# Batch 1's first two row tiles as seven half-size products, and the weight differences for them earlier

## The chip, the core and the metric

The kernel runs on one core of one Trainium2 chip. Such a core has several engines that run their own instruction streams at the same time and meet only at semaphores: TensorE (matrix products; PE in the profile, with PEld for its weight loads), VectorE (DVE), ScalarE (ACT), GpSimd (POOL) and SyncE (SP, which here issues DMAs). Products land in PSUM, which has eight banks; all other tiles are in SBUF. The metric is the device time of one execution in microseconds (us). It was 298.46 us before the change, the median of three runs from 298.05 to 299.08.

## The reference, cut to what matters

The program is block-sparse attention followed by a mixing layer, for four batches of 768 tokens, eight heads of 64.

```python
scores = scale * np.matmul(q, k.transpose(0, 1, 3, 2))
scores = np.where(mask, scores, -1000000000.0)      # blocks: window, first, last, sampled
attn = np.exp(scores - max); attn = attn / attn.sum()
x = np.matmul(attn, v)                              # [4, 768, 512] over all heads
a1 = alpha1 * x + beta1
u = x + lam * np.einsum('ts,bsd->btd', w_tok, a1)   # tokens mixed
a2 = alpha2 * u + beta2
ch = np.maximum(a2 @ w_ch1, 0.0) @ w_ch2            # 512 -> 2048 -> 512
out = u + lam * ch
```

The change is about the last product, `relu(...) @ w_ch2`, with 2048 rows of weights and 512 columns.

## The kernel before, in words

**Units and groups.** A batch has four pairs of heads, so there are 16 pairs, numbered from 0. For each pair the scores are computed transposed (keys on the partitions) in nine *units* of 128 x 1024; a unit's scores are matrix products on TensorE (L601), an exp on ScalarE (L619), from pair 5 on a multiplication by the 0/1 mask on VectorE (L636, "mask" below), and then the products with v on TensorE (L671, "PV", 12 matmuls for one set of keys of one head). A PV accumulates in the single bank named `op`. When all of a head is there, VectorE takes the reciprocal of the sums (L688) and writes the scaled result to x (L689), which frees that bank. GpSimd, for the last head VectorE, then computes a1 (L705, L706).

**The layer's jobs.** Once a batch is ready, its layer is done in small jobs. An *f* (`job_f1`, L919) is four matmuls of 384 columns into one PSUM bank and a Relu on ScalarE (L926), which writes one of 16 rows of h for one half of the tokens; the halves are called c = 0 (token tiles 0, 1, 2) and c = 1 (tiles 3, 4, 5). A *g* (`job_f2`, L1058) is four matmuls of 512 columns, a quarter of the second product of one token tile; the fourth is followed by an addition to x on VectorE (L1067) and a store (L1071, issued by SP). A token product (`job_tok2`, L846) is followed by an addition (L858) and casts (L865) on VectorE.

**The order is written out by hand.** From pair 5 on, each string of W1, W2, W2L and W3 is one *group* of three units. Group n below is the n-th string of W1 followed by W2 and W2L, counted from 0; so groups 0 to 8 belong to pairs 5 to 7, groups 9 to 20 to pairs 8 to 11 and groups 21 to 32 to pairs 12 to 15. Each letter is one step, emitted in that order: `q` the products of the group's three units and the first exp, `x` one further exp, `k` one mask, `p` one PV, `f` and `g` one job of that kind, `T` a token product, `A` two rows of a difference of weights (`job_t`), `S` a sum or difference of rows of h (`job_s`), and others for loads and transposes. The engines execute their own instructions in the order in which these letters put them; nothing is reordered afterwards. An `f` with no job ready does nothing.

**PSUM banks.** Three banks (`mm`) serve the f, g, T, and the first unit of each group (two banks at once); two pairs of banks (`sp`) serve the other two units. A new user of a bank waits for the last reader of the user before it: for an f that is the Relu, for a score unit the exp, for a g the addition.

**Half-size products.** Batches 2 and 3 already compute part of the second product for two token tiles at once, as a quad (`job_p`, L1170): the two tiles by the two halves of the 2048 rows, against w2's four quarters, with seven products of half the columns in place of eight (the Winograd form of Strassen's method). One such product is eight matmuls of 256 columns. It needs four differences of w2's quarters, T1 to T4 (`job_t`, L1098, 16 VectorE instructions in all, in the space of q and k tiles that are no longer used), and four sums or differences of the rows of h (`job_s`, L1144: S1 and S2 write new tiles, S3 and S4 overwrite h). Each of the seven products is followed by an addition to x on VectorE (L1180). Products 1, 6 and 5 share a bank one after the other, and so do 7 and 4. The two tiles of a quad are t and t + 3.

Of the kernel before, what the change touches and what calls it, by code (L numbers as in the profile page):

```python
# [18 lines left out]
B = 4  # L19
H = 8  # L20
S = 768
# [4 lines left out]
DM = 512  # L26
P = 128
NT = S // P
# [13 lines left out]
POUR = [-19, 2, 2]  # L42
W1 = [
# [9 lines left out]
]  # L53
W2 = [
# [12 lines left out]
]  # L67
W2L = [
# [18 lines left out]
]  # L87
STR = (2, 3)
HN = NH // 2
HC = DM // 2  # L90
FS = 6
# [157 lines left out]
def kernel(  # L249
# [16 lines left out]
    nc = tc.nc  # L266
# [194 lines left out]
    def sp_tile():  # L461
        return psum.tile([P, 2, 512], FP, name="sp", tag="sp", bufs=2)
# [111 lines left out]
    x_sbs = {}  # L574
# [234 lines left out]
    did = set()  # L809
# [3 lines left out]
    hts = {}  # L813
# [301 lines left out]
    def a_of(b, t, name, r=slice(0, HN)):  # L1115
        if name in ("X1", "X2"):
            return xs[(b, t, name)][:, r]
        c, half = {"11": (0, 0), "12": (0, 1), "21": (1, 0), "22": (1, 1)}[name]
        return hts[(b, c)][:, HN * half + r.start : HN * half + r.stop, ts(t, P)]

    SOP = {
        1: ("X1", "21", "22", ALU.add),
# [5 lines left out]
    def job_s(b, t, n, r=slice(0, HN)):  # L1128
        dst, a, c, op = SOP[n]
        rows = range(r.start, r.stop)  # L1130
        for name in (a, c):
            if name[0] == "X":
                assert all(("S", b, t, int(name[1]), m) in did for m in rows)
            else:
                h, half = divmod(int(name) - 11, 10)
                assert all(("f", b, h, HN * half + m) in did for m in rows)
# [7 lines left out]
        nc.vector.tensor_tensor(  # L1144
            out=a_of(b, t, dst, r), in0=a_of(b, t, a, r), in1=a_of(b, t, c, r), op=op
        )
        did.update(("S", b, t, n, m) for m in rows)
# [8 lines left out]
        7: ("21", "T3", 3),  # L1156
    }
    banks = {}

    def mul(b, t, n, ps, start, cols=slice(0, HC)):  # L1160
        a, m, need = PROD[n]
        assert m in bq or all((m, r) in did for r in range(0, HN, 2))
        if need:
            assert all(("S", b, t, need, r) in did for r in range(HN))
        c, half = {"1": (0, 0), "X": (1, 0)}.get(a[0], (1, 0))
        if need == 0:
            h, half = divmod(int(a) - 11, 10)
            assert all(("f", b, h, HN * half + r) in did for r in range(HN))
        for r in range(HN):
            nc.tensor.matmul(  # L1170
                ps,
                a_of(b, t, a)[:, r],
                b_rows(m, r)[:, 0, cols],
                start=(start and r == 0),
                stop=(r == HN - 1),
                skip_group_check=True,
            )

    def plus(x, ps):
        nc.vector.tensor_tensor(out=x, in0=x, in1=ps, op=ALU.add)  # L1180

    def twice(ps):
        return ps.unsqueeze(1).broadcast_to([P, 2, HC])

    lo, hi = slice(0, HC), slice(HC, DM)

    def job_p(b, t, n):
        x = x_sbs[b]
        last = (b, t) == (B - 1, NT // 2 - 1)
        bk = banks.setdefault((b, t), {})  # L1190
        if n in (1, 2, 7):
            bk[n] = sp_tile()[:, 0] if n == 1 else mm_tile()[:]
        if n == 3 and not last and 2 not in bk:
            bk[2] = mm_tile()[:]
        if n == 1:
            mul(b, t, 1, bk[1][:, lo], True)
            plus(x[:, t, lo], bk[1][:, lo])
        elif n == 2:
            mul(b, t, 2, bk[2][:, lo], True)
            if last or b < B - 1:  # L1200
                plus(x[:, t, lo], bk.pop(2)[:, lo])
            if last:
                emit_store(b, t, lo)
        elif n == 6:
            mul(b, t, 6, bk[1][:, lo], False)
            plus(x[:, t + 3, lo], bk[1][:, lo])
        elif n == 7:
            mul(b, t, 7, bk[7][:, lo], True)
            plus(x[:, t + 3, hi], bk[7][:, lo])
        elif n == 5:  # L1210
            mul(b, t, 5, bk[1][:, lo], False)
            plus(x[:, t : t + 4 : 3, hi], twice(bk[1][:, lo]))
        elif n == 4:
            mul(b, t, 4, bk[7][:, lo], False)
            plus(x[:, t + 3, lo], bk[7][:, lo])
            emit_store(b, t + 3, slice(0, DM))
        elif last:
            for h in range(2):
                sl = slice(HC + h * P, HC + h * P + P)
                ps = (mm_tile(), op_tile([P, DM]))[h]  # L1220
                mul(b, t, 3, ps[:, sl], True, ts(h, P))
                plus(x[:, t, sl], ps[:, sl])
                emit_store(b, t, sl, (nc.sync, nc.scalar)[h])
        else:
            sl = hi if b < B - 1 else slice(0, DM)
            mul(b, t, 3, bk[2][:, hi], b < B - 1)
            plus(x[:, t, sl], bk[2][:, sl])
            emit_store(b, t, slice(0, DM))
        did.add((b, t, n))

    NPAIR = B * NP
# [34 lines left out]
    def start_mlp(b):  # L1266
# [16 lines left out]
        ]  # L1283
        todo["S"] += [lambda t=t, n=n, r=r: job_s(b, t, n, r) for t, n, r in S_ORDER[b]]

    REST = (6, 7, 5, 4, 3)
    P_ORDER = {
        2: [(0, g, "g") for g in range(4)]
        + [(t, 2) for t in (1, 2)]
        + [(3, g, "g") for g in range(4)]  # L1290
        + [(t, 1) for t in (1, 2)]
        + [(t, n) for t in (1, 2) for n in REST],
        3: [(t, n) for t in range(2) for n in (1, 2)]
        + [(t, n) for t in range(2) for n in REST]
        + [(2, n) for n in (1, 2) + REST],
    }
    ALL, R1, R2 = slice(0, HN), slice(0, HN // 2), slice(HN // 2, HN)
    S_ORDER = {
        2: [(t, n, ALL) for t in (1, 2) for n in (1, 2, 3, 4)],
        3: [(t, n, R1) for n in (1, 2, 3) for t in range(3)]  # L1300
        + [(t, n, r) for t in range(3) for n, r in ((1, R2), (2, R2), (3, R2), (4, ALL))],
    }

    def start_pair(i):
# [227 lines left out]
```

## Time and profile before

| What | us |
|---|---|
| median of the runs | 298.46 |
| the profiled execution, its own time | 298.76 |
| its span in the trace | 297.1 |
| TensorE busy | 289.7 (98%) |
| VectorE busy | 237.8 (80%) |
| ScalarE busy | 217.1 (73%) |
| GpSimd busy | 109.8 (37%) |

The span runs from the first to the last instruction of the trace; the profiled execution's own time is 1.66 us longer. A matmul's end is modelled in this profile and successive matmuls overlap, so TensorE's busy time says less than the distance from one start to the next. The starts of the groups of interest, by their first L601: group 1 at 63.08, group 10 at 105.14, group 15 at 134.56, group 16 at 142.44, group 17 at 148.73, group 18 at 154.89, group 19 at 159.38, group 20 at 164.88, group 21 at 170.21 and group 22 at 173.69 us. In rows of the timeline a bracket at the end gives the idle time of the engine before the instruction and what ended it.

### The profile page before, as it was taken

What the parts mean: (1) busy time and instruction counts of PE and PEld (TensorE: products, weight loads), DVE (VectorE), ACT (ScalarE), POOL (GpSimd) and SP (SyncE); (2) the same over time, 40 slices, a digit from 0 to 9 for tenths busy, and PEclk for the clock granted to TensorE, in tenths of its full rate; (3) what the DMA queues carried; (4) which work ended last, traced back from release to release, by engine and by line L of the source; (5) the groups of instructions that cost most, each with busy time, mean ns of one, the idle gap of its engine ahead of it and who ended that gap; (6) DMA issues with size and microseconds to landing.
All of it is one profiled execution on the core that took longest, in us unless ns stands there. A gap on an engine that the chain in (4) does not pass through costs nothing.

```text
span 297.1 us, 7554 instructions
## 1 busy us (share of the span) xinstructions
PE 289.7 (98%) x3082; PEld 193.5 (65%) x3101; DVE 237.8 (80%) x485; ACT 217.1 (73%) x324; POOL 109.8 (37%) x149
## 2 busy tenths in 40 slices
PE   8999999999999999999999999999999999999995
PEld 3688888665567565565576466556576679665884
DVE  4988899995678796977878777895956899799774
ACT  4999999998899963999779581999869744576000
POOL 8997978632443710355323340335320300000000
PEclk9999999999999999999999999999999999999999
DMA  6999999992392995729955767745520211400032
GB/s 182 184 199 186 192 171 187 171 123 44 95 147 55 112 203 84 118 65 119 125 96 73 124 110 146 103 92 69 70 62 17 38 38 29 141 1 3 0 141 73
DMA packets 57274, 31.09 MB, mean 105 GB/s; under 512 B 37204, under 2 KB 54016, under 8 KB 57240
## 3 DMA queue, kind: packets, MB, share of 16 engines
q0 software_dynamic: 16752, 14.22, 34.4%
q1 hardware_dynamic: 40020, 15.92, 29.3%
q8 instruction: 24, 0.39, 0.6%
q10 hardware_dynamic: 468, 0.47, 0.5%
q14 instruction: 10, 0.08, 0.1%
HBM read 29.75 MB, written 6.29 MB: 121 GB/s over the span
## 4 chain that ended last, share of the span: by engine, by line
PE 84%; DVE 6%; DMA 4%; ACT 3%; issue 1%; POOL 1%; SPq 0%; POOLq 0%
PE mm L919 18%; PE mm L1058 13%; PE sp L601 10%; PE mm L846 8%; PE op L671 7%; PE mm L1170 5%; PE sp L1170 4%; PE mm L601 3%; DVE eT L636 3%; PE mm L822 3%; PE op L648 2%; DMA vr<-in_v_dram 2%; ACT eT L619 2%; PE mm L1016 2%; PE sp L1016 2%; DMA uraw<-ubf 2%
## 5 line engine op out<-in xcount | busy, mean ns | idle before, releaser
L619 ACT ACTIVATE eT<-sp,expb 128x1024 f16<-128x1024 f32 x111 | 118.4, 1120 | 2.1 <-PE sp L601 1.4
L636 DVE TENSOR_TENSOR eT<-eT,mask 128x1024 f16<-128x1024 f16 x99 | 80.6, 843 | 13.5 <-ACT eT L619 13.3
L919 PE MATMUL mm<-uT,w1b 128*128 128x384 bf16 x416 | 76.8, 326 | 0.4 <-ACT hts L926 0.3
L705 POOL TENSOR_TENSOR a1pp<-x_sb,vbc 128x384 bf16<-128x384 f32 x25 | 28.5, 1138 | 119.0 <-DVE x_sb L689 84.7
L619 ACT ACTIVATE eT<-mm,expb 128x512 f16<-128x512 f32 x66 | 41.7, 685 | 26.5 <-PE mm L601 26.3
L926 ACT ACTIVATE hts<-mm 128x384 bf16<-128x384 f32 x104 | 49.1, 502 | 13.3 <-PE mm L919 12.4
L919 PEld LDWEIGHTS <-w1b 128*128 128x128 bf16 x416 | 38.7, 98 | 26.4 <-issue 2.9
L1058 PE MATMUL mm<-w2b,hts 128*128 128x512 bf16 x205 | 52.2, 379 | 0.9 <-issue 0.2
L671 PEld LDWEIGHTS <-eT 128*128 128x128 f16 x792 | 29.8, 98 | 8.8 <-issue 1.7
L1058 PEld LDWEIGHTS <-hts 128*128 128x128 bf16 x224 | 19.8, 98 | 22.3 <-issue 3.9
L671 PE MATMUL op<-vext,eT 128*128 128x65 f16 x792 | 32.1, 194 | 0.4 <-DVE x_sb L689 0.3
L601 PE MATMUL sp<-qTs,kTs 88*128 88x512 bf16 (+1 forms) x120 | 26.9, 325 | 1.2 <-ACT eT L619 0.7
L706 POOL TENSOR_TENSOR a1pp<-a1pp,vbc 128x384 bf16<-128x384 bf16 x25 | 26.7, 1069 | 2.0
L846 PE MATMUL mm<-a1pp,wtokT 128*128 128x256 bf16 x216 | 25.9, 273 | 0.1
L846 PEld LDWEIGHTS <-wtokT 128*128 128x128 bf16 x216 | 20.6, 98 | 5.6 <-issue 1.8
L1170 PEld LDWEIGHTS <-hts 128*128 128x128 bf16 x208 | 19.5, 98 | 3.0 <-issue 0.3
L858 DVE TENSOR_TENSOR x_sb<-x_sb,mm 128x512 f32<-128x512 f32 x18 | 12.3, 686 | 9.9 <-PE mm L846 9.8
L601 PE MATMUL sp<-qhT,khT 64*128 64x256 bf16 (+1 forms) x176 | 19.8, 322 | 0.0
L601 PEld LDWEIGHTS <-khT 64*128 64x128 bf16 x264 | 10.6, 94 | 12.7 <-issue 9.2
L648 PEld LDWEIGHTS <-eT 128*128 128x128 f16 x360 | 14.9, 97 | 3.8 <-issue 0.3
L689 DVE TENSOR_TENSOR x_sb<-op,rcp 128x384 f32<-128x384 f32 x28 | 15.6, 558 | 1.0
L1067 DVE TENSOR_TENSOR x_sb<-x_sb,mm 128x512 f32<-128x512 f32 x14 | 9.6, 686 | 8.2 <-PE mm L1058 6.7
(135 smaller groups left out, 376.9 us busy)
## 6 DMA issues: line engine op xcount, KB each, us to landing
out_dram<-x_sb SPq DMA_DIRECT2D x23, 256.0 KB
qpad<-in_q_dram POOLq DMA_DIRECT2D x15, 192.0 KB, 4.6
kr<-in_k_dram POOLq DMA_DIRECT2D x15, 192.0 KB, 5.3
vr<-in_v_dram POOLq DMA_DIRECT2D x15, 192.0 KB, 6.3
w1b<-in_moe_w_ch_dram POOLq DMA_DIRECT2D x4, 512.0 KB, 9.2
w2b<-in_moe_w_ch_dram POOLq DMA_DIRECT2D x4, 512.0 KB, 7.7
hts<-in_moe_w_tok_dram POOLq DMA_DIRECT2D x2, 576.0 KB, 8.7
x_sb<-in_k_dram ACTq DMA_DIRECT2D x2, 192.0 KB
```

What stands on the lines that cost most here:

```text
L601: nc.tensor.matmul(sp[jj][:, dst], lhsT, rhs, start=True, stop=True, skip_group_check=True,)
L619: nc.scalar.activation(dst, at, AF.Exp, bias=expb[:], scale=SCALE)
L636: nc.vector.tensor_mul(out=e, in0=e, in1=keep)
L648: nc.tensor.matmul(op[0][:, o, :], ets[u][:, jj, h * QB + n * P : h * QB + n * P + P], vexts[i % NVB][:, w, 2 * jp + jj, :], start=op[1] == 0,
L671: nc.tensor.matmul(op[0][:, o, :], ets[u][:, jj, h * QB + n * P : h * QB + n * P + P], vexts[i % NVB][:, w, 2 * jp + jj, :], start=op[1] == 0,
L705: eng.tensor_tensor(out=dst, in0=x_sbs[b][:, :, cols], in1=bc[0], op=ALU.mult)
L706: eng.tensor_tensor(out=dst, in0=dst, in1=bc[1], op=ALU.add)
L846: nc.tensor.matmul(ps[:, o], wtokT[:, os_, ts(2 * n + o, P)], a1pps[i][:, os_, :], start=(os_ == 0 and o == 0), stop=(os_ == NT - 1 and o ...
L919: nc.tensor.matmul(ps[:, 0:QC], w1b[:, dk, ts(n, P)], uTs[b][:, dk, ts(c, QC)], start=(dk == 0), stop=(dk == 3),)
L926: nc.scalar.activation(h_row(b, c, n), ps[:, 0:QC], AF.Relu)
L1058: nc.tensor.matmul(ps[:], ht[:, nk, ts(o % 3, P)], w2b[:, nk, :], start=(nk == 0), stop=(nk == NH - 1),)
L1170: nc.tensor.matmul(ps, a_of(b, t, a)[:, r], b_rows(m, r)[:, 0, cols], start=(start and r == 0), stop=(r == HN - 1), skip_group_check=True,)
```

## The change

Batch 1 joins the batches with half-size products, with one quad of its tiles 0 and 1; tiles 2 to 5 stay as they were. A quad is now named by its two tiles, so that both may lie in the half c = 0; the quads of batches 2 and 3 are the same as before under the new names, and product 1 of the new quad uses an `mm` bank where theirs uses an `sp` bank.

- Eight g of batch 1 go (groups 15, 16, 19 and 20), seven half-size products come: product 2 at the end of group 17, products 1 and 6 in group 18, products 5, 7 and 4 in group 19, product 3 in group 20. S1 is in group 15, S2 in group 16, S3 and S4 in group 18.
- The f of batch 1 come earlier: groups 15 and 16 have nine and six in place of seven and four, the last is in group 19 in place of 21, and the g of tile 2 and later are one letter later or earlier.
- The 16 letters A leave groups 14, 15 and 18 for groups 1 (three), 3 (two), 4 (three), 5 (three), 7 (one), 8 (two) and 9 (two).

```diff
 W1 = [
-    "q Y 0 f 1 k p 2 x f f f x f k k p f g",
+    "q Y 0 f 1 k A A A p 2 x f f f x f k k p f g",
...
-    "q K x g p k 0 k 1 x Q p L Y f f g 2 g k",
-    "q g g x x 0 1 f k 2 k f p k p",
-    "q 0 s 1 s k x x p T f 2 k f k p",
+    "q A A K x g p k 0 k 1 x Q p L Y f f g 2 g k",
+    "q A A A g g x x 0 1 f k 2 k f p k p",
+    "q A A A 0 s 1 s k x x p T f 2 k f k p",
...
-    "q f 0 1 x s f T 2 f L d k k x f k f p p",
-    "q 0 x p x g k k 1 d g k g 2",
+    "q f 0 1 x s f T 2 f L d k A k x f k f p p",
+    "q A A 0 x p x g k k 1 d g k g 2",
 ]
 W2 = [
-    "q 0 p p g k x L x p f k 1 K 2 k",
+    "q A A 0 p p g k x L x p f k 1 K 2 k",
...
-    "q k 0 f x f p s f f x 1 L p k 2 f f f k Y A A A A A f",
-    "q f L f 0 f k A A A A A A A A 1 f Y x f p g x f p f g k k 2",
-    "q x k x k Q 0 g 1 s f f g p 2 p f f k p",
-    "q T 0 k f 1 x k f T x f 2 p k K p",
-    "q A A A x 0 x T k 1 k f 2 k f Q f d p L",
-    "q x 0 x K k g d k s f g f 1 k p p g 2",
-    "q Y g x x k g k f 0 1 k 2 p g v g v",
+    "q k 0 f x f p s f f x 1 L p k 2 f f f k Y f",
+    "q f L f 0 f k 1 f f S Y x f p f x f p f k k 2",
+    "q x f k x f k Q 0 1 s f f p 2 p f f k S p",
+    "q T 0 k f 1 x k f T x f 2 p k K p g",
+    "q S S g x 0 x T k g 1 k f 2 k f Q d p L",
+    "q x 0 x K k g d k s g f 1 k p p g 2",
+    "q Y g x x k g k 0 1 k 2 p v g v",
 ]
 W2L = [
-    "q 0 p p g k x L x p f k 1 K 2 k",
+    "q 0 p p g k x L x p g k 1 K 2 k",
...
-STR = (2, 3)
+STR = (1, 2, 3)
...
+    LATE = [(2, (1, 4)), (2, (2, 5))] + [(3, (o, o + 3)) for o in range(3)]
...
-        if n in (1, 2, 7):
-            bk[n] = sp_tile()[:, 0] if n == 1 else mm_tile()[:]
+        if n == 1 and (b, t) in LATE:
+            bk[1] = sp_tile()[:, 0]
+        elif n in (1, 2, 7) or (n == 3 and not tail):
+            bk[n] = mm_tile()[:]
...
     P_ORDER = {
+        1: quad((0, 1), (2, 1, 6, 5, 7, 4, 3)) + direct(2, 3, 4, 5),
...
     S_ORDER = {
+        1: [((0, 1), n, ALL) for n in (1, 2, 3, 4)],
```

The letter `g` stands for the next of the batch's second-product jobs, whichever kind it is.

More of the change, by code (lines that the diff above doesn't have):

```diff
@@ L1117, in a_of, with a_ready @@
             return xs[(b, t, name)][:, r]
-        c, half = {"11": (0, 0), "12": (0, 1), "21": (1, 0), "22": (1, 1)}[name]
-        return hts[(b, c)][:, HN * half + r.start : HN * half + r.stop, ts(t, P)]
+        o, half = t[int(name[0]) - 1], int(name[1]) - 1
+        return hts[(b, o // 3)][:, HN * half + r.start : HN * half + r.stop, ts(o % 3, P)]
+    def a_ready(b, t, name, rows):
+        if name[0] == "X":
+            return all(("S", b, t, int(name[1]), m) in did for m in rows)
+        o, half = t[int(name[0]) - 1], int(name[1]) - 1
+        return all(("f", b, o // 3, HN * half + m) in did for m in rows)
     SOP = {
@@ L1130, in job_s @@
         rows = range(r.start, r.stop)
[L1131 to L1136, printed above, removed]
+        assert a_ready(b, t, a, rows) and a_ready(b, t, c, rows)
         if n == 3:
@@ L1164, in mul @@
             assert all(("S", b, t, need, r) in did for r in range(HN))
[L1165 to L1168, printed above, removed]
+        assert a_ready(b, t, a, range(HN))
         for r in range(HN):
@@ L1221, in job_p @@
                 mul(b, t, 3, ps[:, sl], True, ts(h, P))
-                plus(x[:, t, sl], ps[:, sl])
-                emit_store(b, t, sl, (nc.sync, nc.scalar)[h])
-        else:
[L1225 to L1228, printed above, removed]
+                plus(x[:, o1, sl], ps[:, sl])
+                emit_store(b, o1, sl, (nc.sync, nc.scalar)[h])
+        else:
+            assert {(b, t, m) for m in (1, 2, 5)} <= did
+            sl, ps = (slice(0, DM), bk[2]) if tail else (hi, bk[3])
+            mul(b, t, 3, ps[:, hi], not tail)
+            plus(x[:, o1, sl], ps[:, sl])
+            emit_store(b, o1, slice(0, DM))
         did.add((b, t, n))
@@ L1284, in start_mlp, with direct, quad @@
         todo["S"] += [lambda t=t, n=n, r=r: job_s(b, t, n, r) for t, n, r in S_ORDER[b]]
+    def direct(*tiles):
+        return [(o, g, "g") for o in tiles for g in range(4)]
+    def quad(t, order):
+        return [(t, n) for n in order]
     REST = (6, 7, 5, 4, 3)
     P_ORDER = {
[L1288 to L1295, printed above, removed]
+        1: quad((0, 1), (2, 1, 6, 5, 7, 4, 3)) + direct(2, 3, 4, 5),
+        2: direct(0)
+        + quad((1, 4), (2,))
+        + quad((2, 5), (2,))
+        + direct(3)
+        + quad((1, 4), (1,))
+        + quad((2, 5), (1,))
+        + quad((1, 4), REST)
+        + quad((2, 5), REST),
+        3: quad((0, 3), (1, 2))
+        + quad((1, 4), (1, 2))
+        + quad((0, 3), REST)
+        + quad((1, 4), REST)
+        + quad((2, 5), (1, 2) + REST),
     }
     ALL, R1, R2 = slice(0, HN), slice(0, HN // 2), slice(HN // 2, HN)
+    Q3 = [(0, 3), (1, 4), (2, 5)]
     S_ORDER = {
[L1299 to L1301 removed]
+        1: [((0, 1), n, ALL) for n in (1, 2, 3, 4)],
+        2: [(t, n, ALL) for t in ((1, 4), (2, 5)) for n in (1, 2, 3, 4)],
+        3: [(t, n, R1) for n in (1, 2, 3) for t in Q3]
+        + [(t, n, r) for t in Q3 for n, r in ((1, R2), (2, R2), (3, R2), (4, ALL))],
     }
```

26 lines of the change are left out of this document (13 added, 13 removed).

## The prediction

> **What bounds the kernel now.** I read the engine totals, then busy time by stretch, then the rows in order of time around the change. Group n is the n-th string of W1 followed by W2, counted from 0; f, g and PV are the jobs named in the section on the kernel. From the page's engine totals and the busy time by stretch (columns: stretch, its length, busy us of PE, PEld, DVE, ACT, POOL with instruction counts, clock, DMA share, GB/s):
>
> ```profile
> PE 289.7 (98%) x3082; PEld 193.5 (65%) x3101; DVE 237.8 (80%) x485; ACT 217.1 (73%) x324; POOL 109.8 (37%) x149
> ```
> ```profile
> 63.08:105.14 42.06, 41.85 (x441) 25.29 (x445) 31.14 (x55) 37.54 (x57) 18.24 (x20) 1.00 0.72 95
> 134.56:154.89 20.33, 20.23 (x203) 12.91 (x204) 15.45 (x33) 16.29 (x27) 7.87 (x9) 1.00 0.94 124
> ```
>
> The first stretch is groups 1 to 9, the second groups 15 to 17. TensorE has almost no idle time in either, at full clock, while VectorE and ScalarE have a fifth of the second free. The profile models where a matmul ends, so I price each kind by its pace, start to start, in the chain that ended last (start us, length us, what):
>
> ```profile
> 54.76 1.30 PE mm L919 x8
> 114.19 1.73 PE mm L1058 x8
> 251.13 0.87 PE sp L1170 x8
> ```
>
> That is 0.163 us for 384 columns, 0.216 for 512, 0.109 for 256: an f (four) is 0.65, a g (four) 0.86, a half-size product (eight) 0.87. The timeline of groups 15 and 16 shows these paces without holes:
>
> ```profile
> 135.32 3.42 PE L919 MATMUL mm<-uT,w1b 128*128 128x384 bf16 x20
> 138.58 0.53 PE L671 MATMUL op<-vext,eT 128*128 128x65 f16 x12
> 138.95 1.02 PE L1058 MATMUL mm<-w2b,hts 128*128 128x512 bf16 x3
> 141.48 1.03 PE L1058 MATMUL mm<-w2b,hts 128*128 128x512 bf16 x4
> 142.44 0.39 PE L601 MATMUL mm<-qhT,khT 64*128 64x512 bf16 x2
> 143.19 1.04 PE L1058 MATMUL mm<-w2b,hts 128*128 128x512 bf16 x4
> ```
>
> Five f take 138.58 - 135.32 = 3.26, a PV of 12 takes 0.37, the scores 0.75, and before the scores 0.09 is lost (142.44 - 141.48 - 0.87). So TensorE's order of work sets the time here: what it is spared counts, and what makes it wait counts too.
>
> **TensorE's saving.** Eight g (32 matmuls of 512) go, 6.91 us; seven products (56 of 256) come, 6.10. Saved: 0.81 us, the most that the change can give. The pace of 0.109 is of the same kind of product, one weight load for each, so the 24 more loads are in it.
>
> **The moved differences.** Sixteen L1098 instructions leave groups 14, 15 and 18. TensorE did not wait for VectorE there, so this gives nothing. In groups 1 to 9 they fill VectorE's gaps:
>
> ```profile
> 82.00 0.69 DVE L1067 TENSOR_TENSOR x_sb<-x_sb,mm 128x512 f32<-128x512 f32 x1 [2.10 <-PE mm L1058]
> 85.66 0.69 DVE L636 TENSOR_TENSOR eT<-eT,mask 128x1024 f16<-128x1024 f16 x1 [1.16 <-ACT eT L619]
> ```
> ```profile
> L1098 DVE TENSOR_TENSOR qTs<-w2b 128x512 bf16<-128x512 bf16 x4 | 1.4, 409 | 0.0
> L1144 DVE TENSOR_TENSOR xs<-hts 128x1024 bf16<-128x1024 bf16 x2 | 1.4, 682 | 0.0
> L1180 DVE TENSOR_TENSOR x_sb<-x_sb,mm 128x256 f32<-128x256 f32 x15 | 6.2, 417 | 1.4 <-PE mm L1170 1.4
> ```
>
> Three of 0.41, overlapping by 0.07, are 1.1 us: inside 2.10 (group 4) and 1.16 (group 5). In the stretch VectorE idles 42.06 - 31.14 = 10.9 us for 5.5 us of added work. I take nothing; a bound is 0.5 us, if one set of three runs late in group 5 and its delay reaches the scores of group 7, which wait for an L858.
>
> **The added VectorE work.** Four sums of 0.68 and seven additions of 0.42 (one of 512 columns, 0.69) replace two of 0.69: 4.5 us more in groups 15 to 20, partly where the differences leave. The matrix sums themselves are early enough. What is late stands in the next three parts.
>
> **First wait: groups 15 and 16.** Two g each become f, 0.43 us less for TensorE and two Relus more for ScalarE. From the timeline of ScalarE, and a hand-over where TensorE did wait:
>
> ```profile
> 138.13 0.49 ACT L926 ACTIVATE hts<-mm 128x384 bf16<-128x384 f32 x1 [0.16 <-PE mm L919]
> 138.52 1.11 ACT L619 ACTIVATE eT<-sp,expb 128x1024 f16<-128x1024 f32 x1
> 139.51 0.49 ACT L926 ACTIVATE hts<-mm 128x384 bf16<-128x384 f32 x1
> 139.88 1.13 ACT L619 ACTIVATE eT<-sp,expb 128x1024 f16<-128x1024 f32 x1
> 140.88 0.51 ACT L926 ACTIVATE hts<-mm 128x384 bf16<-128x384 f32 x1
> 142.86 1.27 ACT L619 ACTIVATE eT<-mm,expb 128x512 f16<-128x512 f32 x2 [0.69 <-PE mm L601]
> ```
> ```profile
> 127.22 0.49 ACT L926 ACTIVATE hts<-mm 128x384 bf16<-128x384 f32 x1
> 127.77 0.39 PE L601 MATMUL mm<-qhT,khT 64*128 64x256 bf16 x4
> ```
>
> An exp holds ScalarE 1.00 us, a Relu 0.37; a Relu starts 0.20 after its f's last column (137.93 to 138.13) and frees its bank 0.49 + 0.05 later. Changed group 15: scores to 135.32, nine f, two PV: TensorE is at the scores of group 16 at 141.92 + 0.09 = 142.01. Their second product needs the bank of the eighth f. ScalarE: Relu of the fifth f 138.79, exp 139.16, two Relus 140.16 and 140.53, exp 140.90, Relu of the eighth 141.90 to 142.40. TensorE waits to 142.45, 0.42 beyond the 0.03 by which that product follows. In group 16 ScalarE then does two half exps (0.57 each) from 142.64, an exp, a Relu to 145.28; the fourth f needs that bank and stands ready at 145.14: 0.19. Together 0.61. Ends: 0 (the banks come in time) and 0.9.
>
> **Second wait: scores of group 19.** The last f of group 18 now stands one PV ahead of the scores and holds a bank that they use. It is free 0.20 + 0.49 + 0.05 = 0.74 after the f; TensorE asks 0.37 + 0.09 + 0.03 after it: 0.25. Ends 0 and 0.4.
>
> **Third wait: product 4 of group 19.** It waits for the addition of product 7, which on VectorE stands behind a mask, the addition of product 5 and another mask. Rows of before, VectorE and POOL:
>
> ```profile
> 157.17 0.69 DVE L858 TENSOR_TENSOR x_sb<-x_sb,mm 128x512 f32<-128x512 f32 x1 [0.56 <-PE mm L846]
> 158.31 1.89 DVE L636 TENSOR_TENSOR eT<-eT,mask 128x1024 f16<-128x1024 f16 x3
> 160.11 0.19 DVE L688 RECIPROCAL rcp<-op 128x6 f32<-128x6 f32 x1
> 160.34 0.56 DVE L689 TENSOR_TENSOR x_sb<-op,rcp 128x384 f32<-128x384 f32 x1
> 160.97 1.00 POOL L705 TENSOR_TENSOR a1pp<-x_sb,vbc 128x384 bf16<-128x384 f32 x1 [9.22 <-DVE x_sb L689]
> 161.10 3.35 DVE L636 TENSOR_TENSOR eT<-eT,mask 128x1024 f16<-128x1024 f16 x3 [0.21 <-ACT eT L619]
> 162.05 1.25 POOL L706 TENSOR_TENSOR a1pp<-a1pp,vbc 128x384 bf16<-128x384 bf16 x1
> ```
>
> Three masks take 1.89 alone and 3.35 beside POOL's L705 and L706. In the changed order L858 to the end of L689 is 3.72 + 0.33 for the addition put among them, so L705 starts 0.20 + 4.05 + 0.07 = 4.32 after the third token product. The next mask is ready after product 6 (0.87), two f (1.30), a PV (0.37), 0.09, 0.42 to the exp (142.44 to 142.86), its halves 0.57 and 0.69, and 0.03: 4.34. A tie. If L705 starts first, the two masks take 1.49 and 0.83 instead of 0.69, each overlapping its neighbours by 0.09, and the addition of product 7 ends at 4.34 + 1.40 + 0.60 + 0.74 + 0.42 = 7.50; TensorE is there at 2.63 + 1.00 (scores with the second wait) + 0.87 + 0.87 + 0.65 + 0.74 = 6.76, and waits 0.8. If the mask starts first, it waits for nothing. I take the middle, 0.4, since the rows put the two within 0.02 of each other.
> The Trainium skill (SBUF — State Buffer, Who interferes with whom) says that a VectorE instruction with two SBUF inputs and a POOL instruction reading SBUF exclude each other, and whichever issues first holds the port for its whole length; the 3.35 against 1.89 agrees. By that rule the sum has 0 or 0.8 here, never the middle, and comes to +0.65 or +1.45.
>
> **Fourth wait: group 21.** Group 20 shrinks on TensorE, but its exps and masks stay. Before:
>
> ```profile
> 164.88 0.39 PE L601 MATMUL mm<-qhT,khT 64*128 64x256 bf16 x4
> 165.30 1.26 ACT L619 ACTIVATE eT<-mm,expb 128x512 f16<-128x512 f32 x2 [1.43 <-PE mm L601]
> 166.46 2.12 ACT L619 ACTIVATE eT<-sp,expb 128x1024 f16<-128x1024 f32 x2
> 167.31 1.99 DVE L636 TENSOR_TENSOR eT<-eT,mask 128x1024 f16<-128x1024 f16 x3
> 169.22 0.19 DVE L688 RECIPROCAL rcp<-op 128x6 f32<-128x6 f32 x1
> 169.45 0.56 DVE L689 TENSOR_TENSOR x_sb<-op,rcp 128x384 f32<-128x384 f32 x1
> 170.96 0.91 PE L671 MATMUL op<-vext,eT 128*128 128x65 f16 x24
> ```
>
> The PV of group 21 needs the single op bank, which L689 frees behind the group's last mask: 170.01 - 164.88 = 5.13 after the scores began, fixed by exps and masks. TensorE came at 6.08. Now it does scores 0.75, product 3 0.87, two g 1.73, PV 0.37, 0.09, scores 0.75 = 4.56, and waits 0.05 + 0.57 = 0.6. Ends 0.3 and 0.8.
>
> **Queues.** SP's store of tile 0 (issued in group 16 before) moves behind product 3 in group 20; a k transpose behind it goes earlier, nothing later. POOL's order is unchanged. From group 22 on all order is as before, so a shift stays to the end.
>
> **Sum.** -0.81 + 0.61 + 0.25 + 0.4 + 0.6 = +1.05 us. The profiled execution took 298.76 (span 297.1 and 1.66 around it), 0.30 above the median 298.46; on the median this is 299.5.
>
> **Rivals.**
> (1) TensorE's saving is kept whole: 298.46 - 0.81 = 297.65. For it: ScalarE has 4.0 us free in groups 15 to 17, four Relus are 1.5. Against it: the waits are of order, not of load. It decides if L689 of group 20 comes within 4.6 us of the scores and the Relu of the eighth f before the second exp; all waits together must stay under 0.81.
> (2) The mask of group 19 starts before L705: no third wait, +0.65, 299.1. The rows leave it open by 0.02. (The Trainium skill's rule above makes this a case by itself, not a shade of the forecast.)
> (3) VectorE falls behind: sums S2 or S3 meet POOL's L705 as the masks did, each 0.7 longer, before the additions that release products 1, 6 and 4: 1 us more, 300.5. Against it: L705 is due in the other part of these groups.
> (4) The early differences cost 0.5 in group 7: 300.0.
>
> **Chances.** Forecast 0.42, (1) 0.15, (2) 0.25, (3) 0.13, (4) 0.05. A change of 0.3% (0.9 us) is about what a measurement of this kernel can tell from none: below 297.56 faster, above 299.36 slower. Faster only from the low edge of (1), 0.04. Same: 0.11 of (1), 0.17 of (2), 0.15 of the forecast, 0.43. Slower 0.53. Range 298.1 to 300.4, which leaves out most of (1) and half of (3); the forecast with its own bounds is 298.9 to 300.2.
>
> **What would show it.** Right: 32 L1058 fewer, 56 half-size more at 0.109; TensorE waiting at the scores of groups 16 and 19 for Relus, at a half-size product in group 19 for an addition and at the PV of group 21 for L689; the scores of group 22 some 1 us later than 173.69 if group 15 starts as before. Wrong: no such gaps, or a start of group 15 later than 134.56.

## The result and the profile after

The changed kernel takes 300.22 us, the median of six runs from 299.94 to 300.46; beside it the kernel before took 298.66 (six runs, 298.05 to 299.08). The ratio is 1.0049 with a 95% interval of 1.0038 to 1.0061: slower by 0.5%. The prediction was 299.5 with a range from 298.1 to 300.4, on a median of 298.46. The profiled execution of the changed kernel took 300.24, with a span of 298.5.

The engine totals of the changed kernel's page, to be read against those of before (289.7, 237.8 and 217.1):

```profile
PE 291.0 (97%) x3125; PEld 196.1 (66%) x3125; DVE 242.4 (81%) x494; ACT 217.3 (73%) x324; POOL 109.8 (37%) x149
```

TensorE's share reads 97% in place of 98%, but that is rounding: 291.0 of 298.5 and 289.7 of 297.1 are both 97.5%. Its busy time rose by 1.3 us although 0.81 us of matmuls went, because this profile draws a matmul that waits as a longer one (the two L601 of group 16 take 0.83 below, those of group 21 0.39). So the totals don't show the waits. Where they are, is told by the starts of the groups, the first L601 of each, in the two profiled executions:

| Group | before, us | after, us | after minus before |
|---|---|---|---|
| 10 | 105.14 | 105.18 | +0.04 |
| 15 | 134.56 | 134.60 | +0.03 |
| 16 | 142.44 | 142.04 | -0.39 |
| 17 | 148.73 | 148.57 | -0.16 |
| 18 | 154.89 | 155.61 | +0.71 |
| 19 | 159.38 | 161.19 | +1.81 |
| 20 | 164.88 | 167.11 | +2.23 |
| 21 | 170.21 | 170.94 | +0.73 |
| 22 | 173.69 | 175.22 | +1.54 |
| 23 | 184.40 | 186.32 | +1.92 |
| 25 | 191.54 | 193.46 | +1.92 |
| 26 | 196.74 | 198.24 | +1.50 |
| 32 | 235.51 | 237.01 | +1.50 |

Up to group 15 nothing happened, from group 26 on nothing more. Between them the groups hold different work in the two kernels, so a single difference is not yet a wait. The waits are read from the changed kernel's timeline of TensorE, against the paces of the prediction (an f 0.65, a product 0.87, a PV 0.37, the scores 0.75, 0.09 ahead of a group):

```profile
142.04 0.83 PE L601 MATMUL mm<-qhT,khT 64*128 64x512 bf16 x2
142.51 0.80 PE L601 MATMUL sp<-qhT,khT 64*128 64x256 bf16 x6
143.24 2.99 PE L919 MATMUL mm<-uT,w1b 128*128 128x384 bf16 x16
146.07 0.90 PE L671 MATMUL op<-vext,eT 128*128 128x65 f16 x24
...
161.19 0.65 PE L601 MATMUL mm<-qhT,khT 64*128 64x512 bf16 x2
...
162.21 1.05 PE L1169 MATMUL mm<-qTs,xs 128*128 128x256 bf16 x8
...
164.62 0.90 PE L671 MATMUL op<-vext,eT 128*128 128x65 f16 x24
166.14 1.03 PE L1169 MATMUL mm<-kTs,hts 128*128 128x256 bf16 x8 [0.62 <-DVE x_sb L1179]
...
170.94 0.39 PE L601 MATMUL mm<-qhT,khT 64*128 64x512 bf16 x2
...
172.29 0.91 PE L671 MATMUL op<-vext,eT 128*128 128x65 f16 x24 [0.53 <-DVE x_sb L689]
...
175.22 0.39 PE L601 MATMUL mm<-qhT,khT 64*128 64x512 bf16 x2
...
176.38 1.89 PE L1058 MATMUL mm<-w2b,hts 128*128 128x512 bf16 x8 [0.34 <-ACT eT L619]
```

(A wait inside a run of equal instructions has no bracket; it shows as a distance that is too long.) The scores of group 16 take 143.24 - 142.04 = 1.20, 0.45 too long, and its four f 2.83 in place of 2.60, 0.23 too long: the first wait is 0.68. The scores of group 19 take 1.02: the second is 0.27. Product 4 starts at 166.14 where two PV from 164.62 end at 165.36: the third is 0.78. The PV of group 21 is due at 170.94 + 0.75 = 171.69 and starts at 172.29: the fourth is 0.60. And the first g of group 22 starts 1.16 after the scores in place of 0.75: a fifth wait of 0.41, for an exp, that the prediction did not have. (That exp's first half, which frees one bank, starts at 175.65; the g follows it at 176.38.) In group 25 the changed kernel gets 0.42 back (1.92 to 1.50). The four waits less the saving are 0.68 + 0.27 + 0.78 + 0.60 - 0.81 = 1.52, and group 22 starts 1.54 late; the last two nearly cancel.

The rows of VectorE and GpSimd behind the third wait, changed kernel:

```profile
162.91 1.52 DVE L636 TENSOR_TENSOR eT<-eT,mask 128x1024 f16<-128x1024 f16 x1
164.36 0.67 DVE L1179 TENSOR_TENSOR x_sb<-x_sb,mm 128x512 f32<-128x512 f32 x1
164.95 0.81 DVE L636 TENSOR_TENSOR eT<-eT,mask 128x1024 f16<-128x1024 f16 x1
165.68 0.41 DVE L1179 TENSOR_TENSOR x_sb<-x_sb,mm 128x256 f32<-128x256 f32 x1
...
162.89 1.00 POOL L705 TENSOR_TENSOR a1pp<-x_sb,vbc 128x384 bf16<-128x384 f32 x1 [11.29 <-DVE x_sb L689]
163.96 1.25 POOL L706 TENSOR_TENSOR a1pp<-a1pp,vbc 128x384 bf16<-128x384 bf16 x1
```

L705 started at 162.89 and the mask at 162.91. The mask then took 1.52, and the addition of product 7 (the last L1179) ended at 166.09, 0.05 before product 4.

### The profile page after: what moved, and what is told of

The parts are those of the page before. It is cut to its first block, busy times and chain, and to the rows that moved or that the text cites. A ratio compares the mean times of both kernels' runs of the same rounds, so it can differ in the third digit from the quotient of the medians.

```text
span 298.5 us, 7632 instructions
## 1 busy us (share of the span) xinstructions
PE 291.0 (97%) x3125; PEld 196.1 (66%) x3125; DVE 242.4 (81%) x494; ACT 217.3 (73%) x324; POOL 109.8 (37%) x149
## 4 chain that ended last, share of the span: by engine, by line
PE 85%; ACT 7%; DVE 5%; issue 1%; DMA 1%; ACTq 0%
PE mm L919 20%; PE mm L1058 13%; PE sp L601 10%; PE mm L846 8%; PE op L671 7%; PE mm L1169 6%; ACT eT L619 5%; PE sp L1169 4%; PE mm L601 3%; PE mm L822 3%; PE op L648 2%; PE mm L1016 2%; DVE eT L636 2%; PE sp L1016 2%; PE mm L648 1%; ACT hts L926 1%
## 5 line engine op out<-in xcount | busy, mean ns | idle before, releaser
L705 POOL TENSOR_TENSOR a1pp<-x_sb,vbc 128x384 bf16<-128x384 f32 x25 | 28.5, 1139 | 120.5 <-DVE x_sb L689 86.2
L1058 PE MATMUL mm<-w2b,hts 128*128 128x512 bf16 x192 | 46.7, 379 | 0.3 <-ACT eT L619 0.3
L1058 PEld LDWEIGHTS <-hts 128*128 128x128 bf16 x192 | 17.0, 98 | 18.9 <-issue 3.2
L601 PE MATMUL sp<-qTs,kTs 88*128 88x512 bf16 (+1 forms) x120 | 26.9, 325 | 1.1 <-ACT eT L619 0.7
L706 POOL TENSOR_TENSOR a1pp<-a1pp,vbc 128x384 bf16<-128x384 bf16 x25 | 26.7, 1068 | 2.0
L1169 PEld LDWEIGHTS <-hts 128*128 128x128 bf16 x248 | 23.2, 98 | 4.8 <-issue 1.8
L858 DVE TENSOR_TENSOR x_sb<-x_sb,mm 128x512 f32<-128x512 f32 x18 | 12.3, 685 | 10.6 <-PE mm L846 10.5
L601 PE MATMUL sp<-qhT,khT 64*128 64x256 bf16 (+1 forms) x176 | 20.2, 323 | 0.0
L601 PEld LDWEIGHTS <-khT 64*128 64x128 bf16 x264 | 10.9, 94 | 13.1 <-issue 9.8
L689 DVE TENSOR_TENSOR x_sb<-op,rcp 128x384 f32<-128x384 f32 x28 | 15.6, 557 | 1.0
L1179 DVE TENSOR_TENSOR x_sb<-x_sb,mm 128x256 f32<-128x256 f32 (+2 forms) x25 | 11.0, 443 | 4.0 <-PE mm L1169 3.7
```

Source lines behind the costliest of these rows:

```text
L601: nc.tensor.matmul(sp[jj][:, dst], lhsT, rhs, start=True, stop=True, skip_group_check=True,)
L705: eng.tensor_tensor(out=dst, in0=x_sbs[b][:, :, cols], in1=bc[0], op=ALU.mult)
L706: eng.tensor_tensor(out=dst, in0=dst, in1=bc[1], op=ALU.add)
L1058: nc.tensor.matmul(ps[:], ht[:, nk, ts(o % 3, P)], w2b[:, nk, :], start=(nk == 0), stop=(nk == NH - 1),)
L1169: nc.tensor.matmul(ps, a_of(b, t, a)[:, r], b_rows(m, r)[:, 0, cols], start=(start and r == 0), stop=(r == HN - 1), skip_group_check=True,)
```

## Experiments

Times are medians; beside them stands the kernel before as it ran with them.

### Only the moved differences

The kernel before with its sixteen letters A in groups 1 to 9, at the places that the change gives them:

```diff
-    "q g g x x 0 1 f k 2 k f p k p",
+    "q A A A g g x x 0 1 f k 2 k f p k p",
...
-    "q A A A x 0 x T k 1 k f 2 k f Q f d p L",
+    "q x 0 x T k 1 k f 2 k f Q f d p L",
```

> The kernel before, with only the sixteen differences of weights moved to groups 1, 3, 4, 5, 7, 8 and 9; no quad in batch 1, and the order of f and g as before. Theory (the new waits cost the time, the moved differences nothing): 298.7 us, the same as before within 0.2, and every group from 10 on starts within 0.1 us of before. Rival (the early differences delay a cast and with it the scores of group 7): 0.5 us slower, 299.2, with group 8 starting 0.5 us late.

Measured: 298.84 us beside 298.77, ratio 1.0006 (0.9998 to 1.0014). Group 0 starts 0.06 earlier than before (56.72 against 56.78), and groups 8 and 10 do too (97.78 against 97.85, 105.08 against 105.14); so does group 20 (164.81 against 164.88). So the differences cost nothing where they are now, and gave nothing where they were. Rival (4) is out.

### The changed order without the quad

The changed strings, with g in place of the seven products, the eighth g in group 20, and no sums:

```diff
-    "q S S g x 0 x T k g 1 k f 2 k f Q d p L",
+    "q g x 0 x T k g 1 k f 2 k f Q d p L",
...
-    "q Y g x x k g k 0 1 k 2 p v g v",
+    "q Y g x x k g g k 0 1 k 2 p v g v",
...
-STR = (1, 2, 3)
+STR = (2, 3)
```

> The changed kernel's order of f, g and differences in every group, but without the quad of batch 1: its seven products are g again at the same places, and the eighth g stands in group 20; the four sums and their additions are left out. Theory (the waits come from the order, except the third, which comes from the additions): the first, second and fifth wait stay, the third (0.78) goes, the added g (0.87) fills the fourth (0.58): 299.7 us, with group 20 starting 0.78 us before that of the changed kernel. Rival (the products or their sums cost more than the 0.87 each that the profile shows): groups 17 to 19 are shorter as well, and the time is 299.3 or less.

Measured: 299.61 us beside 298.50, ratio 1.0035 (1.0021 to 1.0049). Its trace runs 0.28 ahead of the changed kernel's from group 10 to group 15. Less that, group 20 starts 0.84 earlier than in the changed kernel, group 21 at the same time, and group 22 0.58 earlier: the third wait is not there, and the added g of 0.87 takes the place of the fourth. Two things follow. The order alone, without a single half-size product, costs about 1.1 us. And a product costs TensorE what a g costs: group 18 lasts 5.58 with two products (155.61 to 161.19) and 5.56 with two g (155.32 to 160.88). So the saving is the eighth g.

### The eighth Relu ahead of the exp

```diff
-    "q f L f 0 f k 1 f f S Y x f p f x f p f k k 2",
+    "q f L f 0 f k 1 f f S Y x f p f f x p f k k 2",
```

> The changed kernel with one letter moved in group 15: the eighth f stands ahead of the last exp, so that its Relu does too; TensorE's own order is the same. Theory (the first wait is one of order alone): group 16 starts 0.4 us earlier, at 142.04 still for the first product but with no gap inside its scores, the group after it 0.4 earlier, and the time is 299.8. Rival (ScalarE has nothing free across groups 15 and 16, so the exp that now comes 0.4 later makes the ninth Relu and the exps of group 16 late instead): group 17 starts within 0.15 us of where it did, and the time is 300.1 to 300.3.

Measured: 300.53 us beside 298.77, ratio 1.0056 (1.0044 to 1.0068), no better than the changed kernel's 1.0049. TensorE in group 16 of this kernel:

```profile
142.13 0.39 PE L601 MATMUL mm<-qhT,khT 64*128 64x512 bf16 x2
142.36 0.80 PE L601 MATMUL sp<-qhT,khT 64*128 64x256 bf16 x6
143.15 2.11 PE L919 MATMUL mm<-uT,w1b 128*128 128x384 bf16 x12
145.69 0.81 PE L919 MATMUL mm<-uT,w1b 128*128 128x384 bf16 x4 [0.43 <-ACT hts L926]
146.34 0.90 PE L671 MATMUL op<-vext,eT 128*128 128x65 f16 x24
```

The second product now follows the first at once. But the scores still take 1.02, and the four f take 3.19, of which 0.59 is waiting: 0.86 in all against 0.68. The rival holds: nothing was gained, and the time even lies 0.2 above its range. The likely reason is in ScalarE's timeline of the changed kernel, where no row from 139.20 to the end of the Relus at 148.14 has a bracket; ScalarE is busy 8.80 of these 8.94 us:

```profile
138.81 0.49 ACT L926 ACTIVATE hts<-mm 128x384 bf16<-128x384 f32 x1 [0.16 <-PE mm L919]
139.20 1.11 ACT L619 ACTIVATE eT<-sp,expb 128x1024 f16<-128x1024 f32 x1
...
146.17 1.97 ACT L926 ACTIVATE hts<-mm 128x384 bf16<-128x384 f32 x4
148.31 0.49 ACT L926 ACTIVATE hts<-mm 128x384 bf16<-128x384 f32 x1 [0.16 <-PE mm L919]
```

While ScalarE works without a pause, another order of its work moved the wait and did not remove it.

### Two Relus on VectorE

The Relus of the eighth f of group 15 and of the first of group 16:

```diff
+V_RELU = [(1, 1, 2), (1, 1, 4)]
...
-        nc.scalar.activation(h_row(b, c, n), ps[:, 0:QC], AF.Relu)
+        if (b, c, n) in V_RELU:
+            nc.vector.tensor_scalar_max(
+                out=h_row(b, c, n), in0=ps[:, 0:QC], scalar1=0.0
+            )
+        else:
+            nc.scalar.activation(h_row(b, c, n), ps[:, 0:QC], AF.Relu)
```

> The changed kernel with two Relus on VectorE in place of ScalarE: that of the eighth f of group 15 and that of the first f of group 16. TensorE's order is the same. Theory (the first wait is ScalarE being behind through groups 15 and 16, not the place of one Relu): the gap inside the scores of group 16 (0.42) and the 0.2 among its f go, group 17 starts 0.6 us earlier, and the time is 299.6. Rival (VectorE's masks of these groups are as late, and the two Relus push them and the scaled results behind them): group 17 gains less than 0.2, and the time is 300.1 or more.

Measured: 299.70 us beside 298.50, ratio 1.0045 (1.0029 to 1.0061), with times from 299.41 to 300.60; the profiled execution is the one of 300.60. In it the copy of v that stands ahead of the Relu on VectorE starts at 141.72, when its load has landed, against 140.38 in the changed kernel, so that the Relu starts at 142.00 and the scores wait as before. The other Relu stands behind two masks on VectorE and starts at 145.17, and the fourth f waits 0.48 for it. This one does not decide: the median points to the theory, the trace shows the rival.

### Product 2 in group 15

```diff
-    "q f L f 0 f k 1 f f S Y x f p f x f p f k k 2",
+    "q f L f 0 f k 1 f f S Y x f p f x g p f k k 2",
...
-    "q T 0 k f 1 x k f T x f 2 p k K p g",
+    "q T 0 k f 1 x k f T x f f 2 p k K p",
```

> The changed kernel with product 2, which needs no sum, in group 15 in place of the eighth f, and that f in group 17, behind the one there. ScalarE has one Relu less in groups 15 and 16, and the bank that the scores of group 16 need is freed by an addition on VectorE and not by a Relu behind an exp. Theory (the first wait, 0.61 us over both groups, is ScalarE's Relus behind its exps): the gap in the scores of group 16 goes, that among its f shrinks to 0.2 or less, so that group 18 starts 0.5 us earlier, and the time is 299.7. Rival (as with the two Relus on VectorE, the addition is itself late behind a copy that waits for a load): the gap stays, and the time is 300.1 or more.

Measured: 299.98 us beside 298.57, ratio 1.0047 (1.0032 to 1.0061). In its trace the scores of group 16 have no gap:

```profile
142.26 0.39 PE L601 MATMUL mm<-qhT,khT 64*128 64x512 bf16 x2
...
143.01 2.12 PE L919 MATMUL mm<-uT,w1b 128*128 128x384 bf16 x12
145.44 0.81 PE L919 MATMUL mm<-uT,w1b 128*128 128x384 bf16 x4 [0.30 <-ACT hts L926]
146.09 0.90 PE L671 MATMUL op<-vext,eT 128*128 128x65 f16 x24
...
142.36 0.49 ACT L926 ACTIVATE hts<-mm 128x384 bf16<-128x384 f32 x1 [0.30 <-PE mm L919]
```

The scores take 0.75, the four f 3.08, 0.48 too long. One Relu less on ScalarE has taken 0.20 off the 0.68, not the 0.5 that I expected: group 18 starts 0.19 earlier against the changed kernel, beyond a start of the trace that is 0.02 earlier. Both sides missed: the gap went, but the rest grew. The last row tells part of the reason: of the 0.37 that one Relu less frees, ScalarE spends 0.30 idle until the ninth f is done, and only from there on is it without a bracket, to the end of group 16's Relus at 148.17. The edit also has VectorE free the bank of the scores, so it does not part ScalarE's load from the choice of that bank.

### The addition ahead of the mask in group 19

```diff
-    "q x 0 x K k g d k s g f 1 k p p g 2",
+    "q x 0 x K k g d s g k f 1 k p p g 2",
```

> The changed kernel with one mask of group 19 moved behind the addition of product 7 in VectorE's order; all else is in the same order. Theory (product 4 of group 19 waits 0.78 us because that addition stands behind a mask that GpSimd's L705 and L706 lengthen): the wait before product 4 goes, group 20 starts 0.75 us earlier and the time is 299.5. Rival (VectorE is simply late there, and the mask that now comes later delays the scaled result L689 of the next group): group 20 starts 0.75 earlier, but the PV of group 21 waits that much longer, and the time stays at 300.2.

Measured: 299.77 us beside 298.77, ratio 1.0039 (1.0025 to 1.0053). Group 20 starts at 166.63, 0.52 earlier than in the changed kernel (its trace starts 0.04 later), and every later group keeps that. Timeline of TensorE, and VectorE below it:

```profile
164.68 0.90 PE L671 MATMUL op<-vext,eT 128*128 128x65 f16 x24
165.67 1.03 PE L1169 MATMUL mm<-kTs,hts 128*128 128x256 bf16 x8
...
162.97 1.52 DVE L636 TENSOR_TENSOR eT<-eT,mask 128x1024 f16<-128x1024 f16 x1
164.42 1.20 DVE L1179 TENSOR_TENSOR x_sb<-x_sb,mm 128x512 f32<-128x512 f32 x2
165.53 1.28 DVE L636 TENSOR_TENSOR eT<-eT,mask 128x1024 f16<-128x1024 f16 x2
```

Product 4 waits 0.25 where it waited 0.78. So the wait is the one named, and the rival (the next L689 late by as much) is out. A third of it stays, because the first mask, still ahead of both additions, takes 1.52; so group 20 gained 0.52 and not the 0.75 expected.

### The mask ahead of L705

```diff
-    "q S S g x 0 x T k g 1 k f 2 k f Q d p L",
-    "q x 0 x K k g d k s g f 1 k p p g 2",
+    "q S S g x 0 x T k g 1 k f 2 k Q d p L",
+    "q x 0 x K k g d k s g f f 1 k p p g 2",
```

> The changed kernel with the last f of group 18 moved to group 19, behind the one there; TensorE's work is the same. This takes away the second wait (the Relu ahead of the scores of group 19, 0.25 us), brings the scores of group 19 some 0.9 us earlier against the third token product, so that the mask is ready well before GpSimd's L705 may start, and has TensorE at product 4 as late as before. Theory of the rival with the mask first (whoever starts first decides): the mask takes 0.7 and not 1.5, the third wait goes with the second, 299.2 us. Theory that some mask of the group meets L705 or L706 whichever starts first: product 4 still waits 0.3 or more, 299.5 to 299.7. If neither wait is what I take it for, the time stays at 300.2.

Measured: 299.48 us beside 298.50, ratio 1.0034 (1.0018 to 1.0050). TensorE, VectorE and GpSimd in group 19:

```profile
160.55 0.65 PE L601 MATMUL mm<-qhT,khT 64*128 64x512 bf16 x2
...
161.57 1.05 PE L1169 MATMUL mm<-qTs,xs 128*128 128x256 bf16 x8
...
164.72 0.90 PE L671 MATMUL op<-vext,eT 128*128 128x65 f16 x24
165.45 1.04 PE L1169 MATMUL mm<-kTs,hts 128*128 128x256 bf16 x8
...
162.74 0.68 DVE L636 TENSOR_TENSOR eT<-eT,mask 128x1024 f16<-128x1024 f16 x1
163.34 0.68 DVE L1179 TENSOR_TENSOR x_sb<-x_sb,mm 128x512 f32<-128x512 f32 x1
163.94 0.90 DVE L636 TENSOR_TENSOR eT<-eT,mask 128x1024 f16<-128x1024 f16 x1
...
162.90 1.38 POOL L705 TENSOR_TENSOR a1pp<-x_sb,vbc 128x384 bf16<-128x384 f32 x1 [11.30 <-DVE x_sb L689]
```

The mask starts 0.16 before L705, takes 0.68 in place of 1.52, and it is L705 that takes 1.38 in place of 1.00. Product 4 follows the PV without a wait: the third wait is gone, and group 20 starts 0.70 earlier (at 166.42, in a trace that starts 0.01 later). The 0.08 that is missing is before the second f, which now comes 0.09 late. The second wait did not go, against what I wrote: the f that is left in group 18 still stands one PV ahead of the scores, which again take 1.02.

### A g ahead of the PV in group 21, and a g from group 22 to group 20

The first edit fills the fourth wait with a g that stood just behind it; the second brings TensorE later to that PV, and has the first g of group 22 go on in a bank that it holds:

```diff
-    "q 0 p p g k x L x p g k 1 K 2 k",
+    "q g 0 p p k x L x p g k 1 K 2 k",
```
```diff
-    "q Y g x x k g k 0 1 k 2 p v g v",
+    "q Y g x x k g g k 0 1 k 2 p v g v",
...
-    "q Q 0 g x g f v v s T T x k 1 k p p g g T g g Y d 2 k",
+    "q Q 0 g x g f v v s T T x k 1 k p p g T g g Y d 2 k",
```

> The changed kernel with one g of group 21 emitted before the first PV of that group in place of after it. Theory (TensorE waits 0.58 us there for the scaled result L689 to free the single op bank, and has a g at hand): the wait goes, group 22 starts 0.58 us earlier, and the time is 299.6 if the wait for an exp in group 22 stays as it is. Rival (group 22 is set by ScalarE and VectorE, whose exps and masks do not move): group 22 starts earlier, but its first g waits 0.4 to 0.6 us longer for the exp that frees its bank, and the time is 300.1.

> The changed kernel with one g of group 22 moved to group 20. TensorE then comes 0.87 us later to the PV of group 21, and the first g of group 22 goes on in a bank that it holds, in place of taking one that an exp of the same group must free. Theory (a fourth wait of 0.58 for L689 and a fifth of 0.38 for that exp): both go, group 23 starts 0.95 us earlier, and the time is 299.3, if the 0.42 that the changed kernel gains back in group 25 stays gained. Rival (the exp of group 22 is no wait of its own, and shows only because TensorE is early): only 0.58 goes, 299.6.

Measured, the first: 299.62 us beside 298.77, ratio 1.0027 (1.0014 to 1.0039). Group 22 starts at 174.57, 0.59 earlier than in the changed kernel beyond a start that is 0.06 earlier, and the later groups keep 0.55 of it or more. The second: 299.21 us beside 298.50, ratio 1.0025 (1.0015 to 1.0035), and group 23 starts at 185.34 where the changed kernel has 186.32, 0.98 earlier. Its TensorE in groups 21 and 22:

```profile
171.81 0.39 PE L601 MATMUL mm<-qhT,khT 64*128 64x512 bf16 x2
...
172.56 0.91 PE L671 MATMUL op<-vext,eT 128*128 128x65 f16 x24
...
175.50 0.39 PE L601 MATMUL mm<-qhT,khT 64*128 64x512 bf16 x2
...
176.25 1.90 PE L1058 MATMUL mm<-w2b,hts 128*128 128x512 bf16 x8
```

Both distances are 0.75: the fourth and the fifth wait are gone, and both theories hold to 0.03 us in the starts of the groups. The fifth wait is a wait for a bank, as the order of the letters and the exp that ends it tell. In the kernel before and in the changed one the first g of group 22 opens a tile. Before, an f closes group 21, and the new tile gets that f's bank, behind its Relu. After the change a g closes group 21 and keeps its bank until its addition; the scores of group 22 take the other two, and the new tile must have one of them back from the group's own first exp.

### All waits together

Product 2 in group 15, the f of group 18 ahead of product 6 and in group 19, and the g in group 20; in a second kernel the first Relu of group 16 also ahead of its exp, and the second f of group 19 behind a PV. Strings of groups 15 to 20 in the second kernel; group 22 as in the last diff:

```diff
-    "q f L f 0 f k 1 f f S Y x f p f x f p f k k 2",
-    "q x f k x f k Q 0 1 s f f p 2 p f f k S p",
-    "q T 0 k f 1 x k f T x f 2 p k K p g",
-    "q S S g x 0 x T k g 1 k f 2 k f Q d p L",
-    "q x 0 x K k g d k s g f 1 k p p g 2",
-    "q Y g x x k g k 0 1 k 2 p v g v",
+    "q f L f 0 f k 1 f f S Y x f p f x g p f k k 2",
+    "q f x k f x k Q 0 1 s f f p 2 p f f k S p",
+    "q T 0 k f 1 x k f T x f f 2 p k K p",
+    "q S S g x 0 x T k f g 1 k 2 k Q d p L",
+    "q x 0 x K k g d k s g f 1 k p f p g 2",
+    "q Y g x x k g g k 0 1 k 2 p v g v",
```

> The changed kernel with product 2 in group 15 as in the run beside it, the last f of group 18 in group 19 and the other one ahead of product 6, and one g of group 22 in group 20. If the five waits are independent and each goes where it was moved from (0.6 of the first, 0.27 of the second, 0.70 of the third, 0.97 of the fourth and fifth), the time is 297.7 us, 0.8 below the kernel before: the saving on TensorE is then there in full. If a wait that goes makes room for the next one behind it, 298.2 to 298.6, about the kernel before.

> The kernel of the run with all waits moved, with two letters moved: in group 16 the first f ahead of the exp that stood before it, so that its Relu comes before that exp (TensorE's order is the same), and in group 19 the second f behind one PV, so that it no longer asks for the bank of products 1, 6 and 5 before the addition of product 5 is through. Theory (that kernel still waited 0.35 for a Relu in group 16 and 0.35 for an addition in group 19, and nothing else stands behind them): both go, group 23 starts 0.7 us earlier, and the time is 297.5 us, about 1.0 below the kernel before. Rival (the exps that come 0.4 later in group 16 delay its masks and PV, and the scaled result of group 20 is next in group 21): 0.3 of it at most, 297.9.

Measured, the first: 298.14 us beside 298.57, ratio 0.9986 (0.9976 to 0.9995). The second: 297.91 beside 298.53, ratio 0.9984 (0.9975 to 0.9993). Both are a little faster than the kernel before, and both missed their expected time by 0.4, on the side of the rival. The first still waited 0.48 in group 16 and 0.36 in group 19. In the second 0.11 of the wait in group 19 is left, before product 4, but that in group 16 only went behind the PV (two PV from 145.33 end at 146.07, 0.47 before the next row):

```profile
142.72 2.77 PE L919 MATMUL mm<-uT,w1b 128*128 128x384 bf16 x16
145.33 0.90 PE L671 MATMUL op<-vext,eT 128*128 128x65 f16 x24
146.54 1.46 PE L919 MATMUL mm<-uT,w1b 128*128 128x384 bf16 x8 [0.30 <-ACT hts L926]
```

The same happened with the eighth Relu. As in the run with product 2 in group 15, ScalarE idles 0.30 until its ninth Relu, here at 142.07, and has no bracket from there to the end of group 16's Relus at 147.87.

## Why the prediction was right, and by how much it was short

The direction and the range held, at the upper edge: 300.22 is 0.02 above the forecast's own upper bound of 300.2. Step by step:

- **TensorE's saving, 0.81.** Right in size: 32 L1058 went (their weight loads fall from 224 to 192), 56 half-size matmuls came, and group 18 shows two products at the length of two g (5.58 against 5.56).
- **The moved differences, nothing.** Right, measured alone: 1.0006. Rival (4) falls with it.
- **First wait, 0.61.** It measured 0.68, at the places named. The walk found group 16 at 142.01; it started at 142.04 in a trace 0.04 later. The reason given there, the order of two Relus, was too narrow, and so was "the waits are of order, not of load": of the 13.97 us of groups 15 and 16 in the changed kernel ScalarE is busy 12.95. Three runs point to that load: another order left the wait at 0.86 in place of 0.68 or put it behind the PV, and one Relu less left 0.48. But no run removed this wait, so its cause is argued and not shown.
- **Second wait, 0.25.** It measured 0.27. It went in the two runs with all waits moved, where the f stands ahead of product 6.
- **Third wait, 0.4.** This is the step that failed. It measured 0.78, the upper end of 0 or 0.8. The chain was right, down to the start of L705 and the mask within 0.02 us of each other; "I take the middle" was not, since neither order gives the middle. The run with the mask 0.16 us ahead has no wait at all, so the other branch, rival (2), was as real as the one that happened. The Trainium skill (SBUF — State Buffer, Who interferes with whom) has a VectorE instruction with two SBUF inputs and a GpSimd instruction that reads SBUF exclude each other, with the first to issue holding the port; the prediction noted that the sum by it would be +0.65 or +1.45 and never between. Both runs agree: 1.52 for the mask when L705 was first, 1.38 for L705 when the mask was. The mask's 0.84 more stands beside 0.98 that L705 still had to run, and L705's 0.38 more beside 0.52 that the mask still had.
- **Fourth wait, 0.6.** It measured 0.60, and a g ahead of that PV takes 0.59 off the time.
- **"From group 22 on all order is as before, so a shift stays to the end."** Wrong twice, and the two cancel; that the sum needs no term for them is luck. The letters were the same, the banks were not: the last f of batch 1 had left group 21, and with it the bank that the first g of group 22 had been given. That g now waits 0.41 for an exp. And in group 25 there is 0.42 of gain. The kernel before waits there for a transposing load (second L889):

```profile
188.19 1.28 SPq L898 DMA_TRANSPOSE uraw<-ubf  x1
192.81 0.48 DVE L889 TENSOR_SCALAR uT<-uraw,ab2T 128x768 bf16<-128x768 bf16 x1 [0.62 <-DMA uraw<-ubf]
195.25 0.91 PE L671 MATMUL op<-vext,eT 128*128 128x65 f16 x24 [0.25 <-DVE x_sb L689]
```

In the changed kernel, the first two of these:

```profile
190.11 1.26 SPq L898 DMA_TRANSPOSE uraw<-ubf  x1
193.65 0.86 DVE L889 TENSOR_SCALAR uT<-uraw,ab2T 128x768 bf16<-128x768 bf16 x2
```

The load was used 4.6 us after its issue and had been waited for; in the changed kernel it was there within 4.0 us, and the PV of group 25 waits for nothing. Why it lands sooner is open: no run tells it apart. With only the differences moved, the group gained 0.10, and with the changed order without the quad 0.22.

- **The sum.** +1.05 with 0.4 for the third wait is +1.43 with the 0.78 that it measured; the other terms were short by 0.09 together, which makes the 1.52 above. Most of the rest of the miss, 299.5 against 300.22, is the kernel before itself, 298.66 beside the result in place of 298.46.
- **Rival (1), the saving kept whole.** It did not come, and the last run does not bring it either. With the second, fourth and fifth wait gone, 0.11 left of the third and 0.47 of the first, the kernel is 0.62 us below the kernel before (0.9984). Of the saving that leaves 0.81 - 0.47 - 0.11 = 0.23; nearly all the rest is the gain of group 25, which that trace has too (4.79 us from group 25 to 26 in place of 5.20).
- **Rival (3), S2 or S3 beside L705.** It did not happen: in the changed kernel's timeline S2 starts at 147.02 and takes 0.69, S3 at 156.05 and takes 0.68, and GpSimd has no instruction beside either.

## What to carry to other kernels

Where one engine's order sets the time, price a change of work by the waits at the places that it touches: here 0.8 us of spared matmuls brought 2.3 us of waits (0.68, 0.27, 0.78 and 0.60), and the changed order alone, without the cheaper products, cost 1.1. A tie between two instructions that lengthen each other had two outcomes here and none between, so forecast one of them and keep the other as a case. Where an engine works without a pause, do not expect another order on it to remove a wait: here it moved one, and one Relu less only shortened it. A shift that "stays to the end" still has to be walked through the next banks: one job moved away can take with it the bank that the next one was given.

## What was not expected of the hardware

Whether GpSimd's L705 or VectorE's mask starts first decides which of them is lengthened: 0.02 us ahead gave a mask of 1.52 in place of 0.68, 0.16 us behind gave an L705 of 1.38 in place of 1.00. The changed kernel has the second outcome once more: masks from 142.21, an L705 from 142.38 that took 1.36. Additions that read PSUM were not lengthened in the same place: the L1179 of 512 columns took 0.67 beside L706 in the changed kernel and 0.68 beside L705 in the run with the mask first. And loads land at times that no edit near them explains: the same load of v, issued at 137.22 and 137.25, was there for the copy at 140.38 in the changed kernel and at 141.72 in the run with two Relus on VectorE, 1.3 us apart; in the kernel before, issued at 137.19, it was there at 141.24.
